# One row of matmuls per head pair for the products with V, and two casts on another engine

## The chip, the cores and the metric

The kernel runs on one core of a Trainium2 chip. A core has a matrix engine (PE, with its weight loads shown apart as PEld), three engines for elementwise work (DVE, ACT, POOL, that is VectorE, ScalarE and GpSimd) and SP, which here only issues DMAs. Each engine works through its own list of instructions in order; between engines, semaphores say when a piece of data is there. The metric is the device time of one execution in microseconds (us). Before the change it is 854.01 us, the median of three runs (849.0, 854.01 and 856.22).

## The reference

Eight batches of eight heads go through a causal attention with a forgetting bias, and its result through a channel mix. Cut to what is computed:

```
scores = q @ k.T / sqrt(64)                  # 576 x 576 for each of 64 heads
cum    = cumsum(max(s, 0))
scores = where(causal, scores + min(-(cum_q - cum_k), 0), -1e9)
attn   = softmax(scores);  x = attn @ v      # heads side by side: 576 x 512 for each batch
xk, xr = mu * x + (1 - mu) * (x one position earlier)
out    = sigmoid(xr @ w_r) * (max(xk @ w_k, 0)**2 @ w_v)
```

Inputs and output are float32. The kernel gets the precision by splitting numbers into a high and a low part and multiplying three (or four) pairs of parts.

## The kernel before, in words

**Work.** A *visit* is a pair of heads of one batch. The first eight visits (batch 0, in two halves) go an older way through `weighted`; the other 28 (batches 1 to 7, four pairs each) end in `sum_values`. In each visit the heads are called j = 0 and 1. `split_qk` makes the parts of Q and K (tiles G, KH, KL, QL), `split_scores` makes the scores on PE in four PSUM banks (s and t, two each), and on them masks and reduces on DVE (L959), exponentiates on ACT (L974) and writes weights in two float16 halves (ACT L999, DVE L1005) into a tile W. From batch 2 on (`BY_DMA = 2`, 24 visits) SP turns W into the transposed tile T by DMA (`turn_by_dma`, L1082); in batch 1 PE transposes (`turn_by_pe`). There are three buffers for T; a visit uses two.

**Products with V.** `sum_values` (L1175) multiplies V's two float16 parts with the T of both heads. A matmul has 64 output columns for one head, so the two heads go to two halves of the PE array (`tile_position=(0, 64 * j)`) and their matmuls run as a pair. There are 16 such pairs in a visit: twelve for the sums over key blocks (L1200, 192 to 512 moving columns, into the bank po) and four of 64 columns: `ends` (L1218, into po) and `firsts` (L1229, into an s bank called rest). Of these four pairs, the two with V's low part use 64 rows of the array (`k` = 64), all others 128. Two ACT instructions (L1245) then copy po and rest to xT, which goes to DRAM for the channel mix.

**Channel mix.** `channel_mix` takes 256 positions at a time (18 chunks): ACT and DVE mix (L1415, L1422) and split (L1444, L1448), PE multiplies by w_k (L1476), ACT and DVE square and split (L1488 to L1505), PE multiplies by w_r (L1518) and w_v (L1543).

**V and Q.** `split_v` (L707): POOL scales V (L716), ACT rounds it to the float16 high part (L722), POOL subtracts to get the low part (L724). In `split_qk`, ACT rounds Q to G (L805), POOL subtracts to QL (L809); POOL makes K's parts (L790, L794, L800).

**Order.** Nothing runs in the order of the code. Each piece of work is handed to a planner (`Plan`) with its engine, an estimated duration and the buffers it reads and writes; the planner simulates all engines, lets each take the ready piece with the earliest due time, and then emits the instructions of each engine in the order it found. So a piece handed over as one stays in one, and between two pieces anything may be put. In `sum_values` each pair is a piece of its own: the loop hands over 16 pieces to `pe` for a visit, each with its own buffers to wait for.

Of the kernel before, what the change touches and what calls it, by code (L numbers as in the profile page):

```python
# [310 lines left out]
def forgetting_attention_then_channel_mix(  # L311
# [51 lines left out]
    def pe(emit, reads, writes, n, m=P, cycle=1.05 / 2.4, k=P):  # L363
        i = plan.add("PE", n * cycle + (7 if cycle < 0.5 else 2), emit, reads, writes, land=0.83 * m + 1)
        plan.columns[i] = n * k / P * (4 if cycle > 1 else 1)
        return i
# [6 lines left out]
    def act(emit, reads, writes, n, extra=51, table=0, quarters=(0, 0)):  # L373
        return at_quarters(
            plan.add("ACT", n * 0.8333 + extra, emit, reads, writes, land=table), quarters
        )
# [327 lines left out]
        )  # L704
        return V, scales

    def split_v(vn, V, scales):  # L707
        def part(y):
            return V.get()[:, y].rearrange("p k h d -> p (k h d)")

        def whole():
            return vn.get().rearrange("p k h d -> p (k h d)")

        n = P * (NQ + 1)
        pool(
            lambda: nc.gpsimd.tensor_scalar(  # L716
                out=whole(), in0=whole(), scalar1=scales.get()[:, 1:2], scalar2=1.0,
                op0=ALU.mult, op1=ALU.mult,
            ),
            [(scales, 1)], [vn], n, 210,  # L720
        )
        act(lambda: nc.scalar.copy(part(0), whole()), [vn], [(V, 0)], n, 70)  # L722
        pool(
            lambda: nc.gpsimd.tensor_tensor(out=part(1), in0=whole(), in1=part(0), op=ALU.subtract),  # L724
            [vn, (V, 0)], [(V, 1)], n, 210, 2.21,
        )
# [36 lines left out]
    def split_qk(b, hp, qs, k):  # L763

        nq, nk = qs[0].n, k.n
        found = []
        for j in range(2):  # L770
            own, other = slice(64 * j, 64 * j + 64), slice(64 - 64 * j, P - 64 * j)
            QQ, K = (sbuf([P, n], x, 3, F32R) for n, x in ((nq, "G"), (nk, "KH")))
            QL, KB = (sbuf([P, S], x, 3, F32R) for x in ("QL", "KL"))
            if made[0] < 3:
                made[0] += 1
                ahead(lambda QL=QL: nc.vector.memset(f32(QL.get()[64:67]), 1.0), (QL, 1), S)
            dma(
                lambda j=j, KB=KB: nc.sync.dma_start(
                    f32(KB.get()[64:67, 0:nk]), cum3_d.ap[b * H + 2 * hp + j, :, 0:nk]
                ),  # L780
                [(cum3_d, i) for i in range(3)], [(KB, 1)], 40,
            )
            if b < BY_DMA:
                act(
                    lambda own=own, K=K: nc.scalar.copy(K.get()[own], k.get()[own]),
                    [(k, j)], [(K, j)], nk, 90, quarters=(2 * j, 2 * j),
                )
            else:
                pool(
                    lambda own=own, K=K: nc.gpsimd.tensor_copy(K.get()[own], k.get()[own]),  # L790
                    [(k, j)], [(K, j)], nk, 150, 0.8333, (2 * j, 2 * j),
                )
            pool(
                lambda own=own, other=other, K=K: nc.gpsimd.tensor_tensor(  # L794
                    out=K.get()[other], in0=k.get()[own], in1=f32(K.get()[own]), op=ALU.subtract
                ),
                [(k, j), (K, j)], [(K, 1 - j)], nk, 210, 2.21, (2 * j, 2 - 2 * j),
            )
            pool(
                lambda own=own, KB=KB: nc.gpsimd.tensor_copy(KB.get()[0:64, 0:nk], k.get()[own]),  # L800
                [(k, j)], [(KB, 0)], nk, 150, 0.8333, (2 * j, 0),
            )
            x = qs[j]
            act(
                lambda x=x, QQ=QQ: nc.scalar.copy(QQ.get(), x.get()),  # L805
                [(x, 0), (x, 1)], [(QQ, 0), (QQ, 1)], nq, 90,
            )
            pool(
                lambda x=x, QQ=QQ, QL=QL: nc.gpsimd.tensor_tensor(  # L809
                    out=QL.get()[0:64, 0:nq], in0=x.get()[0:64], in1=f32(QQ.get()[0:64]),  # L810
                    op=ALU.subtract,
                ),
                [(x, 0), (QQ, 0)], [(QL, 0)], nq, 210, 2.21,
            )
            found.append(((QQ, K, P), (QL, KB, 67)))
        return found
# [358 lines left out]
    def sum_values(Ts, V, scales, xT):  # L1175

        n = S - 64
        po, rest = bank(1, "po", 1), bank(1, "s", 2)

        def at(y, kb, j):  # L1180
            x = Ts[j][0].get()
            if not y:
                a = n * kb + max(P * kb - 64, 0)
                return x[:, a : n * (kb + 1)]
            t = max(kb, 1)
            a = (t + 1 + kb) * (n // P) + t - 1
            x = x.rearrange("p (x q) -> p x q", q=P)
            return x[:, a : a + (LAST - t) * (n // P + 1) + 1 : n // P + 1]

        def mixed(a, k, j):  # L1190
            return Ts[j][0].get()[:k, n * MIXED + a : n * MIXED + a + 64]


        todo = [(y, x, kb) for kb in range(LAST) for y, x in ((0, 0), (0, 1), (1, 0))]
        for i, (y, x, kb) in enumerate(todo):
            start = max(P * kb - 64, 0) if not y else P * (max(kb, 1) - 1)

            def both(y=y, x=x, kb=kb, start=start, i=i):
                for j in range(2):
                    nc.tensor.matmul(  # L1200
                        po.get()[64 * j : 64 * j + 64, start:n],
                        V.get()[:, x, kb, j],
                        at(y, kb, j),
                        start=i == 0,
                        stop=False,
                        tile_position=(0, 64 * j),
                    )

            before = [(po, ("sum", 0))] if i else []
            pe(  # L1210
                both, [(V, x)] + Ts[0][1](y, kb) + Ts[1][1](y, kb) + before,
                [(po, ("sum", i))] + ([po] if not i else []), n - start, 64, 1.05 / 2.4,
            )
        for x, k in ((0, P), (1, 64)):

            def ends(x=x, k=k):
                for j in range(2):
                    nc.tensor.matmul(  # L1218
                        po.get()[64 * j : 64 * j + 64, n - 64 : n],
                        V.get()[:k, x, LAST, j],  # L1220
                        mixed(n - 64, k, j),
                        start=False,
                        stop=x == 1,
                        tile_position=(0, 64 * j),
                    )

            def firsts(x=x, k=k):
                for j in range(2):
                    nc.tensor.matmul(  # L1229
                        rest.get()[64 * j : 64 * j + 64, 0:64],  # L1230
                        V.get()[:k, x, NQ, j],
                        mixed(n - P, k, j),
                        start=x == 0,
                        stop=x == 1,
                        tile_position=(0, 64 * j),
                    )

            before = [(po, ("sum", y)) for y in range(len(todo) + 1 if x else 1)]
            after = [(po, ("sum", len(todo) + x))] + ([po] if x else [])
            pe(ends, [(V, x)] + Ts[0][1](0, LAST) + Ts[1][1](0, LAST) + before, after, 64, 64, 1.05 / 2.4, k)  # L1240
            pe(firsts, [(V, x)] + Ts[0][1](0, LAST) + Ts[1][1](0, LAST), [rest], 64, 64, 1.05 / 2.4, k)

        for q0, w, ps in ((0, 64, rest), (64, n, po)):
            act(
                lambda q0=q0, w=w, ps=ps: nc.scalar.activation(  # L1245
                    xT.get()[:, 1 + q0 : 1 + q0 + w], ps.get()[:, 0:w], AF.Copy,
                    scale=scales.get()[:, 2:3],
                ),
                [ps, (scales, 2)], [(xT, (0, q0))], w, 130,
            )  # L1250
# [442 lines left out]
    def finish(j, pt, V, xT, n, due):  # L1693
        b, hp, tiles = visits[n]
        plan.due = due
        if n < PLAIN:
            weighted(j, pt, V, xT, tiles)
        else:
            Ts.append(turn_by_dma(pt[0]) if by_dma(n) else turn_by_pe(pt))
            if not j:  # L1700
                if by_dma(n):
                    V = (V[0], *pt[1])
                else:
                    V = (V[0], *laid_out(bank(1, "t", 2), 0, V[1]))
                Vs[n] = V
                split_v(*V)
            else:
                sum_values(Ts[-2:], *Vs[n][1:], xT)
        if j == 1:
# [87 lines left out]
```

## Time and profile before

| | |
|---|---|
| median of three runs | 854.01 us |
| profiled execution, its time | 850.28 us |
| profiled execution, its span | 848.5 us |
| PE / PEld busy | 821.5 / 668.7 us |
| ACT / DVE / POOL busy | 680.1 / 634.0 / 409.3 us |
| mean granted PE clock | 0.980 of full |

The span reaches from the first to the last instruction of the profiled execution; its time is 1.8 us more. An engine's busy time counts a stretch once, however many instructions overlap in it. A matmul's row shows when it starts and for how long it is in flight; matmuls follow one another before the one ahead has ended, so what a matmul costs the engine is read from one start to the next start.

### The profile page before, as it was taken

The numbers are of one execution on the slowest core, as the hardware profiler recorded it, in microseconds if no ns is written. First come the engines' busy times: TensorE is split into PE (matmuls) and PEld (weight loads), VectorE is DVE, ScalarE is ACT, GpSimd is POOL, SyncE is SP. The second block draws the span as 40 slices with busy tenths as digits, with TensorE's granted clock in tenths as the row PEclk, the third lists the DMA queues.
The fourth block names the chain that finished last, engine by engine and source line by source line (L and its number), as shares of the span: only waits on it lengthen the run. The fifth ranks groups of instructions, "written<-read, shape, count | busy, mean of one in ns | idle before, by whom it ended". The sixth has DMA issues, their size and how long they took to land.

```text
span 848.5 us, 17084 instructions
## 1 busy us (share of the span) xinstructions
PE 821.5 (97%) x5214; PEld 668.7 (79%) x5214; DVE 634.0 (75%) x1871; ACT 680.1 (80%) x1999; POOL 409.3 (48%) x549
## 2 busy tenths in 40 slices
PE   9999999996899999999999999999999999999998
PEld 8779788754778787778777787877878888888996
DVE  8978877678787788869787878878877878455431
ACT  6999979679898889889888888889987989445431
POOL 7888988876454545545345555454344431000000
PEclk9989999995899999999999999999999999999999
DMA  7766242248888978877887786787788664410100
GB/s 245 248 213 205 72 132 69 88 132 183 177 173 170 190 155 180 198 163 187 162 181 172 150 190 163 153 200 161 157 191 187 142 124 109 91 50 6 46 26 25
DMA packets 220156, 124.41 MB, mean 147 GB/s; under 512 B 180192, under 2 KB 193504, under 8 KB 220064
## 3 DMA queue, kind: packets, MB, share of 16 engines
q1 hardware_dynamic: 220064, 123.32, 62.6%
q8 instruction: 41, 0.67, 0.3%
q14 instruction: 51, 0.42, 0.2%
HBM read 61.47 MB, written 19.33 MB: 95 GB/s over the span
## 4 chain that ended last, share of the span: by engine, by line
PE 83%; DVE 7%; ACT 7%; issue 2%; DMA 2%; SPq 0%; POOL 0%; ACTq 0%; DVEq 0%; POOLq 0%
PE m L1543 22%; PE m L1476 15%; PE m L1518 10%; PE po L1200 8%; PE s L947 5%; PE t L947 4%; PE po L1346 2%; PE s L857 2%; PE t L1543 2%; PE t L1476 2%; PE s L1476 2%; PE t L1116 2%; PE t L1260 1%; PE s L846 1%; PE s L835 1%
## 5 line engine op out<-in xcount | busy, mean ns | idle before, releaser
L1476 PE MATMUL m<-xh,w_k 128*128 128x256 f32 x976 | 198.1, 290 | 4.6 <-DVE kl L1505 2.3
L1543 PE MATMUL m<-w_v,kh 128*128 128x512 f32 x528 | 177.1, 400 | 0.1
L1476 PEld LDWEIGHTS m<-xh,w_k 128*128 128x128 f32 x976 | 159.9, 193 | 13.1 <-DVE kl L1505 3.6
L1476 PE MATMUL m<-xl,w_k 128*128 128x256 f32 x488 | 141.2, 289 | 0.0
L1543 PEld LDWEIGHTS m<-w_v,kh 128*128 128x128 f32 x528 | 98.2, 188 | 22.3 <-issue 1.7
L1543 PE MATMUL m<-w_v,kl 128*128 128x512 f32 x264 | 105.2, 399 | 0.0
L809 POOL TENSOR_TENSOR QL<-raw,G 64x576 fp32r<-64x576 f32 (+1 forms) x64 | 85.1, 1331 | 36.4 <-ACT G L805 34.2
L1476 PEld LDWEIGHTS m<-xl,w_k 128*128 128x128 f32 x488 | 94.0, 193 | 4.2 <-issue 2.5
L1415 ACT ACTIVATE xp<-x,mu 128x256 f32<-128x256 f32 (+3 forms) x184 | 78.7, 428 | 22.4 <-DMA x<-x_d 13.4
L794 POOL TENSOR_TENSOR KH<-raw,KH 64x576 fp32r<-64x576 f32 x64 | 90.9, 1420 | 3.6 <-POOL W L906 0.3
L1518 PE MATMUL m<-w_r,xh 128*128 128x512 f32 x264 | 90.7, 402 | 0.5 <-ACT t L974 0.3
L1422 DVE SCALAR_TENSOR_TENSOR xp<-x,mu,xp 128x256 f32<-128x256 f32 (+3 forms) x184 | 76.5, 416 | 18.7 <-ACT xp L1415 15.5
L790 POOL CAST KH<-raw 64x576 fp32r<-64x576 f32 x48 | 31.7, 660 | 119.2 <-PE s L947 106.0
L1200 PE MATMUL po<-T,V 128*64 128x512 f16 (+5 forms) x672 | 79.7, 339 | 1.0 <-DMA T<-W 1.0
L1005 DVE SCALAR_TENSOR_TENSOR W<-s,rinv,W 128x192 f16<-128x192 f32 (+2 forms) x144 | 65.3, 456 | 12.1 <-ACT W L999 9.8
L999 ACT ACTIVATE W<-s,rinv 128x192 f16<-128x192 f32 (+2 forms) x144 | 66.2, 463 | 4.0 <-DVE rinv L990 3.1
L1005 DVE SCALAR_TENSOR_TENSOR W<-t,rinv,W 128x320 f16<-128x320 f32 (+1 forms) x96 | 61.8, 645 | 10.1 <-ACT W L999 9.5
L974 ACT ACTIVATE s<-s,nm 128x64 f32<-128x64 f32 (+2 forms) x144 | 62.1, 431 | 8.2 <-DVE nm L959 7.4
L959 DVE CUSTOM_DVE_ANT_0 t<-t,lower 128x320 f32<-128x320 f32 (+1 forms) x96 | 57.5, 601 | 11.3 <-PE t L947 10.4
L999 ACT ACTIVATE W<-t,rinv 128x320 f16<-128x320 f32 (+1 forms) x96 | 58.7, 618 | 2.0 <-DVE rinv L990 1.8
L947 PE MATMUL s<-KH,G 128*128 128x192 f32 (+2 forms) x192 | 52.8, 289 | 7.1 <-DVE W L1005 6.9
L1518 PEld LDWEIGHTS m<-w_r,xh 128*128 128x128 f32 x264 | 49.2, 189 | 12.0 <-DVE kl L1505 0.9
(194 smaller groups left out, 2119.9 us busy)
## 6 DMA issues: line engine op xcount, KB each, us to landing
raw<-in_q SPq DMA_DIRECT2D x112, 144.0 KB
vn<-in_v SPq DMA_DIRECT2D x28, 384.0 KB
raw<-in_k SPq DMA_DIRECT2D x32, 288.0 KB
out<-g SPq DMA_DIRECT2D x36, 256.0 KB
x_d<-xT SPq DMA_DIRECT2D x28, 288.5 KB
x<-x_d SPq DMA_DIRECT2D x11, 514.0 KB
w_k<-in_moe_w_k SPq DMA_DIRECT2D x8, 512.0 KB
w_v<-in_moe_w_v SPq DMA_DIRECT2D x8, 512.0 KB
```

Of the source, the lines that this page charges most:

```text
L794: lambda own=own, other=other, K=K: nc.gpsimd.tensor_tensor(out=K.get()[other], in0=k.get()[own], in1=f32(K.get()[own]), op=ALU.subtract),
L809: lambda x=x, QQ=QQ, QL=QL: nc.gpsimd.tensor_tensor(out=QL.get()[0:64, 0:nq], in0=x.get()[0:64], in1=f32(QQ.get()[0:64]), op=ALU.subtract,),
L947: lambda x=x, G=G, K=K, r=r: nc.tensor.matmul(ps.get()[:m, :n], G.get()[:r, q : q + m], K.get()[:r, k0 : k0 + n], start=x == 0, stop=x == 1,),
L974: lambda: nc.scalar.activation(ps.get()[:, :n], ps.get()[:, :n], AF.Exp, bias=nm.get()[:, i + o : i + o + 1], scale=-1.0, accum_out=sums.g ...
L999: lambda: nc.scalar.activation(part(0), ps.get()[:, :n], AF.Copy, scale=rinv.get()[:, i : i + 1]),
L1005: lambda: nc.vector.scalar_tensor_tensor(out=part(1), in0=ps.get()[:, :n], scalar=rinv.get()[:, i : i + 1], in1=part(0), op0=ALU.mult, op1 ...
L1200: nc.tensor.matmul(po.get()[64 * j : 64 * j + 64, start:n], V.get()[:, x, kb, j], at(y, kb, j), start=i == 0, stop=False, tile_position=(0 ...
L1415: lambda z=z: nc.scalar.activation(to(*z), source(1, *z), AF.Copy, scale=mu.ap[:, which, c + z[0] : c + z[0] + 1]),
L1422: lambda z=z: nc.vector.scalar_tensor_tensor(out=to(*z), in0=source(0, *z), scalar=mu1.ap[:, which, c + z[0] : c + z[0] + 1], in1=to(*z), ...
L1476: lambda u=u, f=f, c=c, n=n, w=w, x=x: nc.tensor.matmul(ps.get()[:, u * CT : (u + 1) * CT], weight["k", c, f // 4].get()[:, w, f % 4 * P : ...
L1518: lambda c=c, n=n, x=x, w=w: nc.tensor.matmul(ps.get(), x.get()[:, c, ts], weight["r", c, 0].get()[:, w], start=c == 0 and n == 0, stop=c ...
L1543: lambda f=f, n=n, x=x, w=w: nc.tensor.matmul(ps.get(), x.get()[:, f, ts], weight["v", f, 0].get()[:, w], start=f == 0 and n == 0, stop=f ...
```

## The change

It has two parts. First, in `sum_values` the 16 pairs of a visit become one piece of work with all buffers to wait for, and the four pairs of 64 columns all use 128 rows of the array. Second, for batches 2 to 7, ACT's rounding of Q to G and of V to its high part is done by POOL.

```diff
-    def split_v(vn, V, scales):
+    def split_v(b, vn, V, scales):
...
-        act(lambda: nc.scalar.copy(part(0), whole()), [vn], [(V, 0)], n, 70)
+        if b < BY_DMA:
+            act(lambda: nc.scalar.copy(part(0), whole()), [vn], [(V, 0)], n, 70)
+        else:
+            pool(lambda: nc.gpsimd.tensor_copy(part(0), whole()), [vn], [(V, 0)], n, 150)
...
-            act(
-                lambda x=x, QQ=QQ: nc.scalar.copy(QQ.get(), x.get()),
-                [(x, 0), (x, 1)], [(QQ, 0), (QQ, 1)], nq, 90,
-            )
+            if b < BY_DMA:
+                act(
+                    lambda x=x, QQ=QQ: nc.scalar.copy(QQ.get(), x.get()),
+                    [(x, 0), (x, 1)], [(QQ, 0), (QQ, 1)], nq, 90,
+                )
+            else:
+                pool(
+                    lambda x=x, QQ=QQ: nc.gpsimd.tensor_copy(QQ.get(), x.get()),
+                    [(x, 0), (x, 1)], [(QQ, 0), (QQ, 1)], nq, 150,
+                )
...
-        def mixed(a, k, j):
-            return Ts[j][0].get()[:k, n * MIXED + a : n * MIXED + a + 64]
+        def mixed(a, j):
+            return Ts[j][0].get()[:, n * MIXED + a : n * MIXED + a + 64]
...
+        def all_of_it():
+            def both(ps, a, e, block, moving, first, last):
                 for j in range(2):
                     nc.tensor.matmul(
-                        po.get()[64 * j : 64 * j + 64, start:n],
-                        V.get()[:, x, kb, j],
-                        at(y, kb, j),
-                        start=i == 0,
-                        stop=False,
+                        ps.get()[64 * j : 64 * j + 64, a:e],
+                        V.get()[:, block[0], block[1], j],
+                        moving(j),
+                        start=first,
+                        stop=last,
                         tile_position=(0, 64 * j),
                     )
...
+            for y, x, kb in todo:
+                both(
+                    po, start(y, kb), n, (x, kb), lambda j: at(y, kb, j), (y, x, kb) == todo[0], False
+                )
+            for x in range(2):
+                both(po, n - 64, n, (x, LAST), lambda j: mixed(n - 64, j), False, x == 1)
+            for x in range(2):
+                both(rest, 0, 64, (x, NQ), lambda j: mixed(n - P, j), x == 0, x == 1)
+
+        keys = [z for T in Ts for y, x, kb in todo + [(0, 0, LAST)] for z in T[1](y, kb)]
+        columns = sum(n - start(y, kb) for y, x, kb in todo) + 4 * 64
+        pe(
+            all_of_it, [(V, 0), (V, 1)] + list(dict.fromkeys(keys)), [po, rest], columns, 64,
+            1.05 / 2.4 + 320 / columns,
+        )
```

On PE, the order of one visit before, from the middle of its sums (po is the bank of the sums, T_1535 and T_199 the transposed weights of the two heads, V_1552 the parts of V):

```order
L1476 MATMUL m_254<-xh_112,w_k_00_461 128x256
L947 MATMUL t_288<-KH_564,G_487 128x320
L947 MATMUL s_153<-KH_564,G_487 128x192
L1200 LDWEIGHTS V_1552
L1200 MATMUL po_88<-T_1535,V_1552 64x512
L1200 LDWEIGHTS V_1552
L1200 MATMUL po_88<-T_199,V_1552 64x512
L947 MATMUL s_153<-KL_645,QL_120 128x192
L1200 LDWEIGHTS V_1552
L1200 MATMUL po_88<-T_1535,V_1552 64x512
```

The same place of a visit in the changed kernel, at the start of its sums and at their end (L956 is what was L947, L1512 what was L1518):

```order
L956 MATMUL t_289<-KH_576,G_483 128x320
L956 MATMUL t_289<-KL_633,QL_120 128x320
L1212 LDWEIGHTS V_1798
L1212 MATMUL po_88<-T_1562,V_1798 64x512
L1212 LDWEIGHTS V_1798
L1212 MATMUL po_88<-T_212,V_1798 64x512
...
L1212 LDWEIGHTS V_1798
L1212 MATMUL s_151<-T_212,V_1798 64x64
L956 MATMUL s_153<-KH_521,G_436 128x448
L956 MATMUL s_153<-KL_543,QL_110 128x448
```

In the whole order before, the 896 matmuls of the 28 visits stand in 120 runs with other work between (44 of the runs are a single pair); in the changed order they stand in 28 runs of 32.

On POOL, one visit of a late batch before (QL, KH, KL are parts of Q and K, vn is V):

```order
L724 TENSOR_TENSOR V_1869<-vn_92,V_1869 128x768
L790 CAST KH_535<-raw_451 64x576
L800 CAST KL_549<-raw_451 64x576
L794 TENSOR_TENSOR KH_535<-raw_451,KH_535 64x576
L809 TENSOR_TENSOR QL_110<-raw_372,G_425 64x576
```

And in the changed kernel, where the rows with L725 and L814 are the moved ones:

```order
L725 CAST V_1798<-vn_90 128x768
L1726 MEMSET xT_194 128x1
L727 TENSOR_TENSOR V_1798<-vn_90,V_1798 128x768
L814 CAST G_436<-raw_378 128x576
L793 CAST KH_521<-raw_445 64x576
L818 TENSOR_TENSOR QL_110<-raw_378,G_436 64x576
L797 TENSOR_TENSOR KH_521<-raw_445,KH_521 64x576
L803 CAST KL_543<-raw_445 64x576
```

The cast that QL needs now stands on the same engine, ahead of the subtraction, and so does the cast of V.

## Rows read from the trace of the kernel before

**Rows 1.** The page: busy time of each engine; the chain that ended last, by engine.

```profile
PE 821.5 (97%) x5214; PEld 668.7 (79%) x5214; DVE 634.0 (75%) x1871; ACT 680.1 (80%) x1999; POOL 409.3 (48%) x549
...
PE 83%; DVE 7%; ACT 7%; issue 2%; DMA 2%; SPq 0%; POOL 0%; ACTq 0%; DVEq 0%; POOLq 0%
```

**Rows 2.** Stretches: length, busy time of PE, PEld, DVE, ACT, POOL, granted clock, DMA.

```profile
190.00:220.00 30.00, 22.52 (x114) 15.86 (x114) 23.89 (x79) 25.82 (x82) 17.01 (x23) 0.66 0.90 179
...
300.00:700.00 400.00, 394.50 (x2576) 319.01 (x2575) 322.90 (x1003) 353.30 (x1090) 188.94 (x206) 1.00 0.79 169
...
740.00:848.50 108.50, 104.76 (x604) 91.15 (x602) 46.02 (x81) 39.95 (x78) 0.00 (x0) 1.00 0.09 30
```

**Rows 3.** Timeline of PE (start, time in flight): a single pair between other work.

```profile
300.39 0.25 PE L947 MATMUL s<-KH,G 128*128 128x192 f32 x1
300.57 0.41 PE L1200 MATMUL po<-T,V 128*64 128x512 f16 x2
300.90 0.35 PE L947 MATMUL s<-KL,QL 67*128 67x192 f32 x1
```

**Rows 4.** Timeline of PE: 28 of a visit's 32 matmuls in one run.

```profile
683.52 0.63 PE L1543 MATMUL m<-w_v,kh 128*128 128x512 f32 x2
683.99 0.39 PE L1543 MATMUL m<-w_v,kl 128*128 128x512 f32 x1
684.31 1.70 PE L1200 MATMUL po<-T,V 128*64 128x512 f16 x16
685.85 0.34 PE L1229 MATMUL s<-T,V 128*64 128x64 f16 x4
686.12 0.63 PE L1200 MATMUL po<-T,V 128*64 128x384 f16 x8
686.68 0.50 PE L947 MATMUL t<-KH,G 128*128 128x512 f32 x1
```

**Rows 5.** Timeline of PE: the last four matmuls of a run, and what follows.

```profile
411.33 0.34 PE L1218 MATMUL po<-T,V 128*64 128x64 f16 x4
411.60 0.49 PE L1518 MATMUL m<-w_r,xh 128*128 128x512 f32 x1
```

**Rows 6.** Timeline of PE: first and last run of a visit with scattered sums.

```profile
567.97 0.62 PE L1200 MATMUL po<-T,V 128*64 128x512 f16 x4
...
579.81 0.37 PE L1218 MATMUL po<-T,V 128*64 128x64 f16 x4
```

**Rows 7.** Waits of PE: who for whom, us in total, times, longest.

```profile
PE t L947 <- DVE W L1005: 2.4, 2, 1.7
...
PE po L1200 <- DMA T<-W: 1.0, 1, 1.0
```

**Rows 8.** Groups of POOL by form: busy, mean ns of one, idle before and its releaser.

```profile
L809 POOL TENSOR_TENSOR QL<-raw,G 64x576 fp32r<-64x576 f32 x56 | 79.3, 1417 | 35.2 <-ACT G L805 33.4
...
L790 POOL CAST KH<-raw 64x576 fp32r<-64x576 f32 x48 | 31.7, 660 | 119.2 <-PE s L947 106.0 <-issue 12.2 <-POOL V L724 0.4
L716 POOL TENSOR_SCALAR vn<-vn,scales 128x768 f32<-128x768 f32 x28 | 25.4, 908 | 3.3 <-DVE scales L698 2.4 <-PE s L857 0.5
```

**Rows 9.** Groups of ACT by form.

```profile
L805 ACT CAST G<-raw 128x576 fp32r<-128x576 f32 x56 | 38.2, 683 | 4.3 <-PE s L947 4.3
...
L722 ACT CAST V<-vn 128x768 f16<-128x768 f32 x28 | 23.6, 842 | 0.0
```

**Rows 10.** Groups of DVE by form, from 300 to 700 us.

```profile
L1505 DVE TENSOR_TENSOR kl<-m,kh 128x512 fp32r<-128x512 f32 x37 | 25.3, 684 | 2.1 <-ACT kh L1503 1.8
```

**Rows 11.** The same, from 740 us to the end.

```profile
L1505 DVE TENSOR_TENSOR kl<-m,kh 128x512 fp32r<-128x512 f32 x4 | 2.7, 687 | 1.3 <-ACT kh L1503 1.3
```

**Rows 12.** Stretches, L1200 alone: busy time of PE and PEld, clock, DMA.

```profile
0.00:220.00 220.00, 17.23 (x120) 5.77 (x120) 0.94 0.56 160
220.00:740.00 520.00, 62.44 (x552) 26.77 (x552) 0.99 0.77 165
```

More of the change, by code (lines that the diff above doesn't have):

```diff
@@ L1188, in at, with start @@
             return x[:, a : a + (LAST - t) * (n // P + 1) + 1 : n // P + 1]
-        def mixed(a, k, j):
-            return Ts[j][0].get()[:k, n * MIXED + a : n * MIXED + a + 64]
+        def mixed(a, j):
+            return Ts[j][0].get()[:, n * MIXED + a : n * MIXED + a + 64]
         todo = [(y, x, kb) for kb in range(LAST) for y, x in ((0, 0), (0, 1), (1, 0))]
-        for i, (y, x, kb) in enumerate(todo):
-            start = max(P * kb - 64, 0) if not y else P * (max(kb, 1) - 1)
-            def both(y=y, x=x, kb=kb, start=start, i=i):
+        def start(y, kb):
+            return P * (max(kb, 1) - 1) if y else max(P * kb - 64, 0)
@@ L1206, in both @@
                         tile_position=(0, 64 * j),
                     )
[L1209 to L1241, printed above, removed]
@@ L1705, in finish @@
                 Vs[n] = V
-                split_v(*V)
+                split_v(b, *V)
             else:
```

## The prediction

> **What bounds the kernel now.** I read the page first, for which engine is busy and which one the chain runs over; then a table of stretches, to see where that holds; then PE's timeline around the sums, for what a matmul costs from one start to the next; and last the groups by form, for the casts that move.
>
> PE is busy for 821.5 of 848.5 us, and 83% of the chain that ended last is PE's; ACT and DVE have 7% each [rows 1]. From 300 to 700 us, where most of the attention runs beside the channel mix, PE is busy 394.5 of 400 us, ACT 353.3, DVE 322.9, POOL 188.9; in the last 108.5 us, where only channel mix is left, PE is busy 104.8 us at full clock [rows 2]. A busy PE is not yet a full one, so I look at starts: two matmuls of 512 columns of the w_v product start 0.47 us ahead of the next, 0.235 us each [rows 4], and 512 columns at 2.4 GHz are 0.213 us. So the array is filled to some 90% there, and what PE is given less of, it finishes sooner. Waits are not the matter: the DMA that brings T costs PE 1.0 us once, the longest wait for DVE's L1005 is 1.7 us [rows 7].
>
> The Trainium skill (Trace Analysis, section Identifying the Most-Contended Engine) says that matmul busy time is a poor measure and that the busy share of the weight loads is a better one. By the page PEld is 79% [rows 1], which by that rule would leave PE a fifth of its time, and the sum below would be worth little. But the share is 91.15 of 108.5 us, 84%, in the last stretch, where PE is the only engine with much to do, and 319 of 400 us, 80%, between 300 and 700 us [rows 2]. Against what a PE with a full queue shows here, that is a slack of 5%, not of 21%.
>
> **The change, part by part.**
>
> *Runs of sums.* A pair of two heads runs side by side, so a pair of 512 columns should cost 0.213 us. Alone between other work it costs more on both sides [rows 3]: the score matmul of 192 columns (0.08 us) starts at 300.39 and the pair only at 300.57, 0.10 us late; the pair starts at 300.57 and the next work at 300.90, that is 0.33 us for 0.213, 0.12 us late. The same 0.11 us shows ahead of a long run (683.99 to 684.31 for 512 columns) [rows 4]. So every change between matmuls of 128 output columns and these of 64 leaves the array empty for about 0.11 us, and a run of sums, long or short, pays 0.22 us. Before there are 120 runs, one visit's spread over 12 us [rows 6]; after there are 28. 92 runs x 0.22 us = **20.2 us** off PE.
>
> *Pairs with 64 rows.* In the middle of a run, four matmuls of 64 columns, one pair with 128 rows and one with 64, take from 685.85 to 686.12, 0.27 us for 0.053 us of columns [rows 4]: going to 64 rows and back costs about 0.22 us. At the end of a run, where the step out is paid anyway, the four take 0.27 us (411.33 to 411.60) [rows 5], less 0.05 for columns and 0.12 for the step out: 0.10 us. There are 56 such islands (two in each of 28 visits), and with all pairs on 128 rows none is left. 56 x 0.10 = 5.6 us is the low end, 56 x 0.22 = 12.3 us the high one; as most of the runs are short, an island mostly ends one, so I take **8 us**. The 64 rows more add no columns; at the most their 56 pairs cost their 0.027 us again, 1.5 us, and I take 0.
>
> *One piece instead of 16.* The row waits for all parts of T and V at once. T is no new wait: the first pair of a visit (key block 0) already reads all four tiles of both heads. V's low part, which half of the pairs could do without so far, is no wait of PE's either: the one that its sums have in the trace is for T [rows 7]. The planner puts other PE work ahead of the row, as it does now ahead of the first pair. Behind the row, though, stand the scores of the next head for its length: 2.37 us for 28 matmuls with one island [rows 4], so about 2.3 us for all 32. PE is at work then, so this costs PE nothing; DVE and ACT live on the other three banks. Cost 0; if that cover fails, it is a rival below.
>
> *Casts.* Off ACT: 24 visits x (2 x 0.683 + 0.842) us [rows 9] = 53 us. Onto POOL: G has 576 elements, V 768. The nearest rows are POOL's cast of 576 elements, 0.660 us, and its scaling of 768, 0.908 us [rows 8]; both give 1.15 to 1.18 ns an element with 64 and with 128 partitions. That makes 0.67 and 0.89 us, and 24 x (2 x 0.67 + 0.89) = 54 us. Between 300 and 700 us POOL goes from 189 to some 230 of 400 us. It loses a wait as well: 33.4 us of idle time in front of QL ended with ACT's G [rows 8]. So POOL has room, and I cost its part at 0: the cover is that Q and K are split a visit (22 us) ahead and that POOL idles half the time. What ACT gets back is off the path as long as PE is the bound. It is worth at most ACT's share of the chain, 7% [rows 1] of 53 us, 3.7 us; I take 0. Without it, ACT at 88% would come near PE once PE needs 5% less.
>
> The Trainium skill (Trace Analysis, section Optimizing Scalar/DVE Operations) warns that GpSimd and VectorE share a port of SBUF, so that work given to one may hold up the other. If each us of the 54 held up DVE for DVE's busy share, 0.81 [rows 2], DVE would lose 44 us. In the trace it does not: with POOL about half busy, DVE's 512-element subtraction at L1505 takes 684 ns [rows 10], with POOL idle 687 ns [rows 11]. I charge nothing.
>
> **The sum.** 20.2 + 8 = 28 us off the profiled execution's 850.3 us: 822 us. The median of the runs stands 3.7 us over it (854.0), so the forecast is **826 us**. Low end of the gain: 83% of (20.2 + 5.6), if a saving counts only where the chain is on PE: 21 us, 833 us. High end: 92 x 0.24 + 12.3 + 3.7 = 38 us, 816 us. The planner lays out everything anew, which may move PE's idle time and the clock by a few us either way; I let the forecast's own range be 812 to 838.
>
> **Rivals.**
>
> *The attention loop sets the pace, not PE.* Scores go PE, DVE, ACT, DVE, ACT through four banks, and ACT at 88% with DVE at 81% may be what ends last; the sums' freed time then turns into PE idle time from 220 to 740 us. For it: 17% of the chain is off PE, and the longest PE waits are for DVE. Against: those waits are a few us in all, and 108 us of channel mix are left at the end to fill PE with. Only the saving in the first 220 us would count, 120 of 672 matmuls of L1200 [rows 12], 18% of 28 = 5 us, and up to 3.7 us of ACT: 845 to 849 us, half of it faster by over 1%.
>
> *The row waits for T (slower).* PE takes its list in order. If the planner's estimate of T's landing is short and the row stands at the head of PE's list, all else stands behind it; before, single pairs of other work broke up that stretch. At 28 / 24 = 1.2 us in each of the 24 visits with T by DMA, the gain is gone; at 1.7 us, the longest such PE wait now [rows 7], it is 41 - 28 = 13 us slower: 867 us. Against it: the first pair waits for the same tiles now, and PE lost 1.0 us to them in all.
>
> *The hole at 190 to 220 us closes.* There PE is busy 22.5 of 30 us at a granted clock of 0.66 [rows 2], between its levels of 1.2 and 2.4 GHz, with ACT busy 25.8. ACT's relief and T set free earlier could give back up to 7.5 us of idle time and some 8 us of half clock: 826 - 15 = 811 us.
>
> That the change doesn't do what it says is excluded by the order: 28 runs of 32.
>
> **Chances.** Forecast 0.68, attention loop 0.18, waiting row 0.06, hole closes 0.08. The range takes in the forecast, the closed hole down to 808 and most of the attention loop: **808 to 848 us**. About 1%, 8.5 us, is what a measurement of this kernel can tell from no change, so faster means below 845.5: 0.68 + 0.08 + half of 0.18 = 0.85; within 1%: 0.09; slower: 0.06.
>
> **What would show it.** Right: PE's span shorter by some 28 us with busy share still at 96% or more; a row of sums of 32 matmuls from first start to next start of about 2.3 us; a change into and out of it of 0.1 us each; casts on POOL of 0.67 and 0.89 us; ACT near 79% between 300 and 700 us. Wrong: PE idle time ahead of the row put down to the DMA of T or of POOL's casts; PE's share of the chain falling well under 83%; score matmuls that wait for DVE more often than now.

## The result, and the profile after

The changed kernel takes **824.02 us** (median of four runs, 821.43 to 825.23); the kernel before took 855.12 us beside it. The ratio is 0.9646, with an interval of 0.9593 to 0.9699. A second measurement on another occasion gave 823.67 against 850.74 us, 0.9675 (0.9636 to 0.9715). The profiled execution takes 824.20 us (before: 850.28), its span 822.5 us. The forecast was 826 us within 808 to 848, so it held. The kernel before has runs of 847 to 852 us, at a mean granted clock of 0.977 to 0.982, and runs of 853 to 859 us at 0.973 or 0.974, so its median moves by some 5 us with how many of each were drawn, and differences against it are read with that in mind.

First the page of the changed kernel: busy time of each engine, and the chain that ended last, by engine.

```profile
PE 789.1 (96%) x5208; PEld 662.1 (80%) x5208; DVE 627.7 (76%) x1871; ACT 640.0 (78%) x1927; POOL 459.0 (56%) x621
...
PE 53%; ACT 16%; DVE 14%; POOL 6%; issue 6%; DMA 4%; SPq 0%; POOLq 0%; ACTq 0%; DVEq 0%
```

Against [rows 1], PE is busy for 32.4 us less and its idle time grows from 27.0 to 33.4 us, so 26.0 us of span are left. ACT is busy 40 us less, POOL 50 us more. PE's share of the chain falls from 83% to 53%, though PE is nearly as full as before (96% for 97%); I come back to that.

Next the stretches of [rows 2], in the changed kernel (length, busy time of PE, PEld, DVE, ACT, POOL, granted clock, DMA share, GB/s).

```profile
190.00:220.00 30.00, 23.38 (x127) 18.61 (x127) 25.71 (x84) 24.15 (x78) 22.39 (x29) 0.66 0.95 205
...
300.00:700.00 400.00, 392.85 (x2662) 330.68 (x2661) 332.13 (x1038) 339.55 (x1078) 225.99 (x258) 0.99 0.82 171
700.00:740.00 40.00, 40.00 (x265) 35.03 (x264) 18.64 (x37) 18.12 (x41) 0.00 (x0) 1.00 0.26 69
740.00:822.50 82.50, 78.71 (x457) 68.57 (x455) 32.34 (x53) 27.76 (x51) 0.00 (x0) 0.99 0.08 26
```

The busy share of PE between 300 and 700 us is nearly unchanged, 98%, but more is done in it: 2662 matmuls for 2576. The last stretch is shorter for it and ends 26 us sooner. From 190 to 220 us little has changed for PE: it is busy 23.4 us for 22.5, at the same clock of 0.66.

A whole row of sums on PE's timeline, which answers to [rows 4]:

```profile
375.47 0.62 PE L1537 MATMUL m<-w_v,kh 128*128 128x512 f32 x2
376.02 2.20 PE L1212 MATMUL po<-T,V 128*64 128x512 f16 x28
378.06 0.23 PE L1212 MATMUL s<-T,V 128*64 128x64 f16 x4
378.22 0.30 PE L956 MATMUL s<-KH,G 128*128 128x64 f32 x1
```

All 32 matmuls of a visit take 2.20 us from first start to next start (376.02 to 378.22), where 28 of them took 2.37 us before.

The casts, now on POOL (count, busy, mean ns of one, idle before and what ended it), beside the subtraction that used to wait for ACT [rows 8]:

```profile
L818 POOL TENSOR_TENSOR QL<-raw,G 64x576 fp32r<-64x576 f32 x56 | 79.4, 1418 | 2.6
...
L814 POOL CAST G<-raw 128x576 fp32r<-128x576 f32 x48 | 31.9, 665 | 73.2 <-issue 42.5 <-PE s L956 28.6 <-POOL xT L1726 0.9
...
L725 POOL CAST V<-vn 128x768 f16<-128x768 f32 x24 | 19.7, 823 | 0.6
```

They take 0.665 and 0.823 us, near the 0.67 and 0.89 that I took from other rows. The 35 us of idle time in front of QL are down to 2.6; POOL now idles in front of the cast instead.

### The profile page after: what moved, and what is told of

Same layout as the page of the kernel before. It is cut to its first block, busy times and chain, and to the rows that moved or that the text cites. A ratio compares the mean times of both kernels' runs of the same rounds, so it can differ in the third digit from the quotient of the medians.

```text
span 822.5 us, 17066 instructions
## 1 busy us (share of the span) xinstructions
PE 789.1 (96%) x5208; PEld 662.1 (80%) x5208; DVE 627.7 (76%) x1871; ACT 640.0 (78%) x1927; POOL 459.0 (56%) x621
## 4 chain that ended last, share of the span: by engine, by line
PE 53%; ACT 16%; DVE 14%; POOL 6%; issue 6%; DMA 4%; SPq 0%; POOLq 0%; ACTq 0%; DVEq 0%
PE m L1537 14%; PE m L1470 9%; PE m L1512 7%; DVE W L1014 3%; PE s L956 3%; PE po L1212 3%; ACT W L1008 3%; ACT t L983 2%; ACT s L983 2%; PE t L1537 2%; PE t L956 2%; PE po L1340 2%; PE t L1470 2%; PE s L1470 2%; DVE t L968 2%
## 5 line engine op out<-in xcount | busy, mean ns | idle before, releaser
L1470 PE MATMUL m<-xh,w_k 128*128 128x256 f32 x976 | 194.7, 289 | 3.6 <-DVE g L1548 2.3
L1512 PE MATMUL m<-w_r,xh 128*128 128x512 f32 x264 | 91.0, 402 | 1.2 <-DVE kl L1499 0.9
L1014 DVE SCALAR_TENSOR_TENSOR W<-s,rinv,W 128x64 f16<-128x64 f32 (+2 forms) x144 | 65.0, 456 | 15.3 <-ACT W L1008 14.1
L814 POOL CAST G<-raw 128x576 fp32r<-128x576 f32 x48 | 31.9, 665 | 73.2 <-issue 42.5
L1008 ACT ACTIVATE W<-s,rinv 128x64 f16<-128x64 f32 (+2 forms) x144 | 65.0, 458 | 7.3 <-DVE rinv L999 6.9
L956 PE MATMUL s<-KH,G 128*128 128x64 f32 (+2 forms) x192 | 54.0, 298 | 14.6 <-DVE W L1014 7.7
L1212 PE MATMUL po<-T,V 128*64 128x512 f16 (+6 forms) x784 | 63.7, 315 | 0.0
L1212 PEld LDWEIGHTS <-V 128*64 128x64 f16 x896 | 43.5, 112 | 25.1 <-issue 5.3
L1442 DVE TENSOR_TENSOR xl<-xp,xh 128x512 fp32r<-128x512 f32 x72 | 49.4, 686 | 16.2 <-ACT xh L1438 15.3
```

What stands on the lines that cost most here:

```text
L956: lambda x=x, G=G, K=K, r=r: nc.tensor.matmul(ps.get()[:m, :n], G.get()[:r, q : q + m], K.get()[:r, k0 : k0 + n], start=x == 0, stop=x == 1,),
L1008: lambda: nc.scalar.activation(part(0), ps.get()[:, :n], AF.Copy, scale=rinv.get()[:, i : i + 1]),
L1014: lambda: nc.vector.scalar_tensor_tensor(out=part(1), in0=ps.get()[:, :n], scalar=rinv.get()[:, i : i + 1], in1=part(0), op0=ALU.mult, op1 ...
L1212: nc.tensor.matmul(ps.get()[64 * j : 64 * j + 64, a:e], V.get()[:, block[0], block[1], j], moving(j), start=first, stop=last, tile_positio ...
L1470: lambda u=u, f=f, c=c, n=n, w=w, x=x: nc.tensor.matmul(ps.get()[:, u * CT : (u + 1) * CT], weight["k", c, f // 4].get()[:, w, f % 4 * P : ...
L1512: lambda c=c, n=n, x=x, w=w: nc.tensor.matmul(ps.get(), x.get()[:, c, ts], weight["r", c, 0].get()[:, w], start=c == 0 and n == 0, stop=c ...
```

## The experiments

Theory: PE is the bound, and the gain is time that PE no longer spends between matmuls of 128 and of 64 output columns (or 128 and 64 rows). Rival: the attention loop through ACT and DVE sets the pace, and room on ACT is the gain.

**1. The row alone.** All casts stay on ACT, that of Q as that of V below.

```diff
-        if b < BY_DMA:
-            act(lambda: nc.scalar.copy(part(0), whole()), [vn], [(V, 0)], n, 70)
-        else:
-            pool(lambda: nc.gpsimd.tensor_copy(part(0), whole()), [vn], [(V, 0)], n, 150)
+        act(lambda: nc.scalar.copy(part(0), whole()), [vn], [(V, 0)], n, 70)
...
```

> One row of 32 matmuls per visit, all casts left on ScalarE. Theory (PE is the bound and the gain is PE time that no longer goes into changing between 128 and 64 output columns): nearly all of the gain, 824 to 832 us. Rival (the attention loop with ScalarE in it sets the pace, and the casts that left it made the room): under half of the gain, 840 us or more.

Measured: 825.02 us (823.04 to 826.63), before 855.0; ratio 0.9654 (0.9588 to 0.9721). Nearly all of the gain, with ACT as busy as before:

```profile
PE 791.2 (96%) x5209; PEld 659.8 (80%) x5209; DVE 627.8 (76%) x1871; ACT 680.0 (82%) x1999; POOL 409.4 (50%) x549
```

The rival is out as an account of the whole.

**2. The casts alone.** The sums stay in 16 pieces; V's cast is shown, Q's is changed in the same way.

```diff
-        act(lambda: nc.scalar.copy(part(0), whole()), [vn], [(V, 0)], n, 70)
+        if b < BY_DMA:
+            act(lambda: nc.scalar.copy(part(0), whole()), [vn], [(V, 0)], n, 70)
+        else:
+            pool(lambda: nc.gpsimd.tensor_copy(part(0), whole()), [vn], [(V, 0)], n, 150)
...
```

> The casts of Q and V from batch 2 on GpSimd, the sums in 16 pieces as before. Theory (PE bound): 850 to 856 us, no change beyond 4 us, since ScalarE is off the path. Rival (ScalarE sets the pace): 840 us or less, for 53 us of its work are gone.

Measured: 844.73 us (843.28 to 846.96), ratio 0.9895 (0.9836 to 0.9954): 4 to 14 us faster. Neither account had this size. Part of it is chance of the order: the planner laid the sums out in 103 runs instead of 120, and 17 runs at 0.22 us (experiment 4) are 3.7 us. The two profiled executions, 846.96 and 850.28 us, are 3.3 us apart, no more than that, and PE's idle time in them has not fallen: 28.2 us of a span of 845.2, for 27.0 us before.

```profile
PE 817.0 (97%) x5216; PEld 670.2 (79%) x5216; DVE 630.1 (75%) x1871; ACT 646.2 (76%) x1927; POOL 458.6 (54%) x621
```

That the rest of the 10 us between the medians is ACT's relief is not shown.

**3. The 64-row pairs alone.** In the kernel before, all pairs on 128 rows.

```diff
-        for x, k in ((0, P), (1, 64)):
+        for x, k in ((0, P), (1, P)):
```

> The kernel before, with all pairs of 64 columns on 128 rows and nothing else changed. Theory: 56 islands of 64 rows cost PE 0.10 to 0.22 us each, so 843 to 850 us. Rival (steps are hidden by waits of other engines): 853 to 857 us, as before.

Measured: 842.28 us (841.26 to 843.29), before 855.0; ratio 0.9864 (0.9807 to 0.9921). The time falls somewhat more than expected, and the interval, 7 to 17 us, is wide. The trace gives a price near the low end of that: PE is busy 812.6 us instead of 821.5, 8.9 us less, although there are 124 runs instead of 120, which at 0.22 us each add 0.9 us. Experiment 5 measures the step itself.

**4. The step by itself, as a dose.** Three extra matmuls of 128 output columns in each of the 28 rows, once inside (`split_3`) and, as a control, three ahead of the row (`front_3`). The diff is that of the first; in the second the three stand in a loop of their own ahead of the sums. They write to unused columns of a bank, and the planner isn't told, so that the rest of PE's order is the same.

```diff
+            def between():
+                nc.tensor.matmul(
+                    rest.get()[:, 128:192], ident16.ap, ident16.ap[:, 0:64],
+                    start=True, stop=True, skip_group_check=True,
+                )
-            for y, x, kb in todo:
+            for i, (y, x, kb) in enumerate(todo):
+                if i in (3, 6, 9):
+                    between()
```

> The changed kernel with three small extra matmuls of 128 output columns (64 moving columns, into unused columns of a bank) put into each of the 28 rows, after the third, sixth and ninth pair; the planner is not told, so all else keeps its order. Each makes PE change to 128 output columns and back. Theory (0.22 us for each way out and back, PE is the bound): 84 x (0.22 + 0.03 to 0.06) = 21 to 24 us more than the changed kernel, 845 to 848 us. Rival (the row's length is hidden behind ScalarE and VectorE): 824 to 830 us.

> The control of the one before: the same three extra matmuls, all ahead of the row, where PE has 128 output columns anyway. Theory: only their own time, 84 x 0.03 to 0.06 = 3 to 5 us, 826 to 829 us. If the extra matmuls themselves cost much (weight loads, the bank), this one rises as the other does.

Measured: 839.28 us (837.2 to 841.11) and 823.40 us (822.96 to 826.51), on the same chip, both less than expected. The medians are 15.9 us apart, for 84 ways out and back 0.19 us each; the two profiled executions (841.11 and 822.96 us) are 18.2 us apart, 0.22 us each. PE's timeline gives the price without that spread. With the extra matmuls inside (L1222 is the extra one):

```profile
407.44 0.84 PE L1212 MATMUL po<-T,V 128*64 128x512 f16 x6
408.21 0.20 PE L1222 MATMUL s<-ident 128*128 128x64 bf16 x1
408.34 0.79 PE L1212 MATMUL po<-T,V 128*64 128x448 f16 x6
409.06 0.20 PE L1222 MATMUL s<-ident 128*128 128x64 bf16 x1
409.19 0.63 PE L1212 MATMUL po<-T,V 128*64 128x320 f16 x6
409.75 0.20 PE L1222 MATMUL s<-ident 128*128 128x64 bf16 x1
409.88 0.53 PE L1212 MATMUL po<-T,V 128*64 128x192 f16 x10
410.24 0.23 PE L1212 MATMUL s<-T,V 128*64 128x64 f16 x4
410.40 0.39 PE L1478 MATMUL m<-xh,w_k 128*128 128x256 f32 x1
```

With them ahead of the row, and the matmul ahead of them:

```profile
397.59 0.28 PE L1478 MATMUL m<-xh,w_k 128*128 128x256 f32 x1
397.71 0.26 PE L1222 MATMUL s<-ident 128*128 128x64 bf16 x3
397.91 2.20 PE L1212 MATMUL po<-T,V 128*64 128x512 f16 x28
```

And the same place in the changed kernel, without them:

```profile
395.19 0.28 PE L1470 MATMUL m<-xh,w_k 128*128 128x256 f32 x1
395.41 2.20 PE L1212 MATMUL po<-T,V 128*64 128x512 f16 x28
```

Inside, the row takes 2.96 us (407.44 to 410.40) for 2.20, 0.76 us more for three. Ahead of the row, the time from the last w_k matmul to the row's start grows from 0.22 us (395.19 to 395.41) to 0.32 us (397.59 to 397.91), so the three themselves cost 0.10 us. (The 0.20 us from 397.71 to 397.91 hold the change into the row as well, which every row pays.) That leaves 0.66 us for three ways out and back, **0.22 us each**, and 84 of them are 18.5 us: of the PE time that was added, 16 to 18 us show in the time of the kernel. That is the cleanest sign that PE is the bound, and no other engine was touched for it. The control adds 28 times 0.10 us, 2.8 us, and yet is not slower than the changed kernel was on other chips (824.02 and 823.67 us); experiment 6 shows a part of why.

**5. The 64-row pairs inside the row.** Same order, every second pair of 64 columns on 64 rows of V and T (the diff shows the two pairs into po; those into rest are alike).

```diff
             for x in range(2):
-                both(po, n - 64, n, (x, LAST), lambda j: mixed(n - 64, j), False, x == 1)
+                k = P - 64 * x
+                both(po, n - 64, n, (x, LAST), lambda j: mixed(n - 64, k, j), False, x == 1, k)
...
```

> The changed kernel with the four pairs of 64 columns as before, every second one on 64 rows: 128, 64, 128, 64 rows at the end of the row, same order otherwise. Theory: three more changes of about 0.11 us in each of 28 rows, 9 us: 831 to 835 us. Rival (changes of the rows are free, or hidden): 822 to 826 us.

Measured: 828.60 us (828.35 to 828.75), 4.6 to 4.9 us over the changed kernel's 824.02 and 823.67 (on other chips); half of what was expected. In the trace the step has its size:

```profile
379.85 2.32 PE L1212 MATMUL po<-T,V 128*64 128x512 f16 x28
382.10 0.37 PE L1212 MATMUL s<-T,V 128*64 128x64 f16 x4
382.39 0.30 PE L956 MATMUL s<-KH,G 128*128 128x64 f32 x1
```

The row takes 2.54 us (379.85 to 382.39), 0.34 more than 2.20, or 0.113 us for each of three steps; 28 rows make 9.5 us. The other half came back somewhere, and that led to the next finding.

**6. Where the casts begin.** The casts on POOL only from batch 3, for Q and for V.

```diff
-        if b < BY_DMA:
+        if b < BY_DMA + 1:
...
```

> The changed kernel, but the casts go to GpSimd only from batch 3; those of batch 2 stay on ScalarE. In the changed kernel the chain of waits lies on GpSimd for 18 us from 180 to 200 us, in the stretch where PE has idle time and a granted clock of 0.66. If GpSimd's queue holds that stretch up, PE gets 5 to 10 us back: 814 to 820 us. If the stretch is held by something else: 822 to 827 us, as the changed kernel.

Measured: 818.95 us (817.05 to 820.53), ratio 0.9590 (0.9533 to 0.9647). The number is the expected one, the reason is not. The stretch that I wanted to relieve is as it was. From 180 to 230 us and from 590 to 620 us, the changed kernel:

```profile
180.00:230.00 50.00, 37.56 (x252) 29.78 (x252) 40.94 (x131) 40.17 (x130) 40.02 (x54) 0.76 0.85 189
...
590.00:620.00 30.00, 28.05 (x190) 23.88 (x189) 21.58 (x63) 22.99 (x69) 19.10 (x21) 0.89 0.81 156
```

and with casts from batch 3:

```profile
180.00:230.00 50.00, 38.13 (x248) 28.14 (x247) 39.31 (x129) 43.88 (x139) 32.52 (x44) 0.76 0.80 176
590.00:620.00 30.00, 29.91 (x211) 24.66 (x208) 23.94 (x75) 25.39 (x83) 17.10 (x19) 1.00 0.77 171
```

In the early stretch POOL is busy 7.5 us less, and PE and its clock gain next to nothing. What differs more is a place 400 us later: from 590 to 620 us, PE is 1.9 us less idle and its clock is 1.00 instead of 0.89. The changed kernel has a stall there. PE's timeline and ACT's at that place (in brackets the idle time ahead of an instruction and what ended it):

```profile
594.09 0.28 PE L1470 MATMUL m<-xl,w_k 128*128 128x256 f32 x1
596.33 0.64 PE L956 MATMUL s<-KH,G 128*128 128x192 f32 x2 [1.95 <-ACT xT L1239]
```

```profile
591.92 0.63 ACT L1008 ACTIVATE W<-s,rinv 128x448 f16<-128x448 f32 x1
594.67 0.48 ACT L1409 ACTIVATE xp<-x,mu 128x256 f32<-128x256 f32 x1 [2.12 <-DMA x<-x_d]
595.09 0.58 ACT L1497 CAST kh<-m 128x512 fp32r<-128x512 f32 x1
595.56 0.47 ACT L1409 ACTIVATE xp<-x,mu 128x256 f32<-128x256 f32 x1
595.97 0.30 ACT L1239 ACTIVATE xT<-s,scales 128x64 f32<-128x64 f32 x1
```

ACT's list stands for 2.12 us at a chunk's first instruction, which waits for its DMA. Three places behind it stands the copy of the sums out of an s bank, and PE's next scores need that bank. So PE waits 1.95 us, and the clock then lies at half for some 7 us:

```profile
596.00:603.00 7.00, 6.67 (x32) 6.68 (x33) 4.73 (x16) 4.08 (x17) 0.79 (x3) 0.51 0.95 247
```

Seven us at half clock cost 3.4 us of work, with the idle time some 5 us in all. The second profile of the changed kernel has the stall again, smaller: 1.78 us of idle time, and a clock of 0.94 from 590 to 620 us, 1.8 us of work. `row_64` has it with 0.98 us and no fall of the clock, and its mean clock is 0.986 for 0.981: that is where the missing 4 to 5 us of experiment 5 are. `front_3` and `split_3` have none, so those two compare fairly; against the changed kernel, the profile of `front_3` has 3.5 us less idle time of PE but the same mean clock, 0.981, so for the control the stall is only a part of the account.

The row alone took 825.02 us beside this run on the same chip, and has no such stall either. So with the casts from batch 3 the kernel is 6 us faster than with none, and with the casts from batch 2 the stall takes most of that back. What the 6 us consist of is not shown. In the profiles (826.63 and 820.15 us) PE is busy for 791.2 us with the row alone and 788.8 us with casts from batch 3, and idle for 33.7 and 29.6 us. But 2.4 us of these 4.1 us of idle time lie ahead of 240 us, where ACT is busy for 210 us in both: the first of the moved casts starts only at 240.2 us. First the row alone, then casts from batch 3:

```profile
0.00:240.00 240.00, 217.95 (x1422) 178.56 (x1423) 193.84 (x582) 209.94 (x602) 186.91 (x308) 0.95 0.60 164
0.00:240.00 240.00, 220.33 (x1433) 180.41 (x1434) 195.50 (x589) 209.97 (x607) 188.12 (x309) 0.94 0.61 165
```

That part comes from another order of work, and not from ACT's relief; behind 240 us, 1.7 us of idle time are left that can be that.

**7. More work in the early hole.** On top of experiment 6, the high-part score matmuls of the first two visits of batch 2 run four times.

```diff
+                    for i in range(1 if x else 1 + again):
                         nc.tensor.matmul(
...
-                            stop=x == 1,
+                            stop=x == 1 or i < again,
```

> The kernel with casts on GpSimd from batch 3, in which the score matmuls of the first two visits of batch 2 (high part) run four times instead of once, each time writing the same numbers anew; order unchanged. They fall into the stretch from 186 to 217 us, where PE has 10 us of idle time and runs at half clock. If that half clock is what the stretch costs and more work lifts it, the time falls by 2 to 6 us from 819 us: 813 to 817 us. If the stretch waits for ScalarE and DMA whatever PE's clock, the time stays or grows by what the extra matmuls take beyond the idle time, 6 x 1600 columns a visit, 0 to 8 us: 819 to 827 us.

Measured: 828.97 us (828.10 to 830.77), above both ranges that were expected, and 9 to 10 us slower than without (818.95 and 820.05 us, on other chips). From 180 to 230 us:

```profile
180.00:230.00 50.00, 39.97 (x250) 32.77 (x249) 34.70 (x114) 38.02 (x119) 26.77 (x39) 0.80 0.72 162
```

The clock rises from 0.76 to 0.80 only, PE is idle for 10.0 us instead of 11.9, and the extra work costs more than it gives. The hole stays: PE waits there for DVE's release of the score banks, 3.84 us at one place:

```profile
192.39 1.44 PE L957 MATMUL t<-KH,G 128*128 128x320 f32 x4 [3.84 <-DVE W L1018]
```

What sets the hole's length was not taken apart further.

**8. On one chip, five rounds.** The changed kernel; casts from batch 3; from batch 4; and from batch 3 with the planner's pace of chunks shortened.

```diff
-    CHUNK = 40600.0
+    CHUNK = 39600.0
```

> The changed kernel once more, unchanged, beside the three below on one chip: its ratio to the kernel before should again be 0.96 to 0.97, some 824 us where the kernel before takes 855 us. If kernels differ between chips by more than between edits, the ratio will say so.

> The casts on GpSimd from batch 3, once more. If its gain over the changed kernel is real, it is again 3 to 7 us under it on the same chip; if the one before was chance of the clock and the chip, it is within 2 us.

> The casts on GpSimd from batch 4 only, those of batches 2 and 3 on ScalarE. If ScalarE has room and only GpSimd's early queue mattered, the same as from batch 3, within 2 us. If each batch's casts on GpSimd still give something, 1 to 3 us slower than from batch 3. With none there (one row alone) it was 825 us.

> From batch 3, and the pace at which the planner is told that chunks of channel mix are due taken from 40.6 to 39.6 us, since PE has 4% less to do in that stretch. If the order's pace leaves PE idle, 2 to 4 us faster than from batch 3; if PE is full either way, within 2 us.

Measured, with the kernel before at 850.74 us: 823.67 (822.49 to 825.35), 820.05 (818.55 to 822.42), 819.66 (818.01 to 822.38) and 818.83 us (814.51 to 822.23). So the gain from batch 3 is real, 3.6 us, and the runs of the two kernels do not overlap, if barely. Batch 3 or 4 makes no difference, so the time does not follow the amount of work that ACT is spared, and the pace gives nothing that can be told apart. The version with casts from batch 3 beats both kernels of this study; its ratio to the kernel before is 0.9632 (0.9588 to 0.9676).

## Why the prediction was right, step by step

*What bounds the kernel.* Right. `split_3` against `front_3`: 18.5 us more on PE, 15.9 us (medians) to 18.2 us (profiled executions) more in the time.

*Runs of sums, 20.2 us.* Right: 92 runs fewer at 0.22 us. The 0.22 us that I had read from a pair's neighbours is what the dose gives.

*Pairs with 64 rows, 8 us.* Right in size. In the trace of the kernel before, the 56 pairs stand in 54 islands; 22 of them lie inside a run and cost two steps, 32 end a run and cost one. That makes 76 steps, at 0.113 us (experiment 5) 8.6 us. The time alone (experiment 3) would say 7 to 17 us, but its order changed too.

*Casts, 0 us.* Right in size for the change as it stands, but by luck, as the sum of a gain and a loss that I had not seen: the row alone takes 825.02 us, with the casts (on other chips) 824.02 and 823.67. From batch 3 the casts come with 6 us less, more than the 3.7 us that I allowed, of which the profiles show some 2 us of idle time that can be ACT's relief (experiment 6). From batch 2 the stall is there as well. DVE was not held up by the 50 us more on POOL: it is busy for 627.7 us, for 634.0 before. On POOL, the changed kernel's waits of PE name no moved cast; those of `casts_only` name the subtraction behind one, once:

```profile
PE t L956 <- POOL QL L818: 3.1, 1, 3.1
```

*One piece, 0 us.* Right for the row: the list of PE's waits holds none of the row's. Its first four lines (who for whom, us in total, times, longest):

```profile
PE s L956 <- DVE W L1014: 7.7, 9, 3.2
PE s L956 <- DVE rinv L999: 4.2, 1, 4.2
PE m L1470 <- DVE g L1548: 2.3, 3, 1.3
PE s L956 <- ACT xT L1239: 2.0, 1, 2.0
```

The last line is the stall of experiment 6. It was not in the sum: 4 to 5 us, lost by a new order of ACT's list.

*The sum.* 20.2 + 8.6 = 28.8 us of PE's time, for the 28 us of the forecast. PE's busy time fell by 32.4 us (by 30.3 with the row alone), its idle time rose by 6.4 (6.7), so the profiled executions are 26.1 us apart, and the medians 27 to 31. The two terms of PE are right by their mechanism. That the time came out as near as it did has some luck in it: idle time, the stall among it, was added and was in no term, and busy time fell by some 4 us more than the two terms, which the runs do not take apart.

*Rivals.* The attention loop did not set the pace. The row did not wait for T. The hole at 190 to 220 us did not close. Of the signs against me, PE's share of the chain went the wrong way, to 53%, and to 56% with the row alone, while the time did what was forecast. I read it so, which no run shows: where several engines are nearly full, the chain goes through whichever of them came last by a hair, and the idle time ahead of PE, 33 of 822 us, says more. The scores' waits for DVE's W are fewer, 10 for 8.0 us instead of 12 for 9.3, but the longest is 3.2 us instead of 1.7, and one of 4.2 us, put down to rinv, is new. All waits of PE for DVE come to 19.3 us; before they were 15.6 us, where I had spoken of a few. The scores' other line before, beside the one in [rows 7]:

```profile
PE s L947 <- DVE W L1005: 6.9, 10, 1.6
```

ACT from 300 to 700 us is at 85%, not at 79%: I had taken the moved casts off, but not put in that more visits would fit into that stretch.

## What to carry to other kernels

When the matrix engine is full, count how often it changes between shapes of its array, not only its columns: here 92 changes there and back, with 76 steps between 128 and 64 rows, were 3% of the time, and a scheduler that doesn't know their price scatters such work. Handing a group of small matmuls over as one piece needs no reason but that, if its inputs all have to be there for the first of them anyway. And check the lists of the other engines after any such reordering: one instruction that waits for a DMA ahead of a bank's release cost 4 to 5 us here.

## What the runs showed of the hardware

A change from matmuls of 128 output columns to these pairs of 64 and back costs PE 0.22 us (`split_3` against `front_3`), and each change between 128 and 64 rows, with the output columns unchanged, 0.113 us (`row_64`). The Trainium skill (TensorEngine Tiling (Array Packing), section Key Properties) says that changing the tiling mode, and not merely the tile, drains the engine; the runs agree, with a loss at each such change, and give the price.

GpSimd's casts take 0.665 us for 128 partitions of 576 elements, and 0.660 us for 64 partitions of as many [rows 8].

After 1.95 us of idle time at 594 us the granted clock, full until then, lay at 0.51 from 596 to 603 us; after 0.98 us at the same place in `row_64` it stayed at 1.00 from 590 to 620 us.
